# A sixth buffer for the evacuated u tiles of a fused SSM and MLP kernel

## The chip, the cores and the metric

The kernel runs on one NeuronCore of a Trainium2 chip. The metric is the time of one execution on the device in microseconds (us); less is better. Seven runs of the kernel before the change took 563.35 to 569.76 us, with a median of 567.07 us.

A core has five engines, each with its own in-order queue of instructions. TensorE (PE) multiplies matrices and writes only PSUM, which here is eight banks of 128x512 float32. ScalarE (ACT) and VectorE (DVE) read PSUM and SBUF. GpSimd (POOL) does small arithmetic on SBUF here and issues DMAs; SyncE (SP) only issues DMAs. All DMAs share the 16 DMA engines of the core. Engines wait for one another, and for DMAs, through semaphores: an instruction that waits holds up everything behind it on its own queue.

## The reference, cut to what matters

```python
def _A_ref(x, ...):                         # a diagonal state-space layer
    Lam_bar = jnp.exp(dt * Lam)
    B_bar = ((Lam_bar - 1.0) / Lam)[:, None] * Bmat
    Bu = jnp.einsum("bld,pd->blp", x + 0j, B_bar)
    for t in range(L):
        h = Lam_bar[None, :] * h + Bu[:, t, :]
        hs.append(h)
    y = 2.0 * jnp.einsum("blp,dp->bld", hseq, Cmat).real + x * Dskip[None, None, :]
def _B_ref(x, w1, b1, w2, b2):              # an MLP on the normalised x
    h = _gelu(jnp.einsum("bsd,df->bsf", _layernorm(x, axis=-1), w1) + b1)
    return jnp.einsum("bsf,fd->bsd", h, w2) + b2
g = _sigmoid((x * gate_w).sum(-1, keepdims=True))
return g * a + (1 - g) * b
```

Here L is 2048 time steps, D and P are 1024, and the MLP is 3584 wide. Everything comes in and goes out as bfloat16.

## The kernel before

**Stages.** TensorE works through four stages. First, u = B x for the real and the imaginary part of B. Then the MLP in eight blocks, "m" (x times w1, GELU) and "b" (h times w2) alternating. Last, "y" (the states times C). The scan over time runs on VectorE beside the MLP: `ssm` (L1214) handles one of 16 units (two halves of P, eight pieces of 256 steps). It loads u from DRAM, rotates it by tables, scans it, rotates it back and stores the states h to DRAM.

**A group.** All but the first few products are made by a scheme with seven products in place of eight (class `SG`, L884). A group of u is one 128-row tile `pt` of B against one half `pr` of x (two pieces of 512 steps); it is 28 matmuls in the products p1, p7, p5, p6, p2, p3 and p4. The loop at L1167 interleaves neighbouring groups: p1 of this group, p7 of the group before, p5, p6, p2, p3 of this group, p4 of the group before. A group uses three PSUM banks: `a` (two banks alternate), `e` (two alternate) and `b` (three rotate). So p1 of group n needs the bank `a` of group n-2, which is free when the u made by p2 of group n-2 has been copied out by ScalarE.

**u buffers.** `bu_group` (L1003) makes 14 groups, numbered 0 to 13 here in the order of L1164: (2,0), (3,0), (0,1), (1,1), (2,1), (3,1), (4,0), (4,1), (5,0), (5,1), (6,0), (6,1), (7,0), (7,1) as (pt, pr). The evacuated u of a group, four pieces of 128x512 bfloat16, goes to one of the 4096-byte buffers of `EVS`, and `EVN` (L948) says which buffer each group takes. `fin` (L1023) evacuates: for piece c = 0 a copy by ScalarE (L1028), for c = 1 an addition by VectorE (L1034, or L1037 and L1039 for the imaginary part). When both pieces of a part `ri` are there, `u_store` (L955) sends 256 KB of it to DRAM through the POOL queue (L958). Buffers 3 and 4 are only used by the four plain products of pt 0 and 1 at the start (L967).

**Held stores.** The normalised x is stored to DRAM (L1094) and read back by four transposing DMAs (L1061, tile `scr_xn`), which wait for the second store of group 4 (L1193). Three stores, both parts of group 5 and the first of group 6, are made to wait until these transposes are done:

```python
for m, ri in ((1, 0), (1, 1), (2, 0)):
    us_t[order[4 + m] + (ri,)].deps |= set(xn_t[:4])
```

**Memory.** `SSM` is 20480 bytes in each partition: three scan buffers of 4096 (`SB0`, L1208) and two work tiles from `SSM + 12288` on (`TM0`). A scan unit loads u into its scan buffer at L1225; units 0, 1 and 2 take the first, second and third. Before the scan starts, the first two of these are also `EVS` 3 and 4.

**Order.** The program calls nothing in a fixed order. It adds tasks with a cost, a priority and the tiles they read and write to a graph (`Graph.add`, L180). A task that writes a tile waits for all earlier readers of it. A list scheduler (L225) simulates the five queues with these costs and fixes the order on each queue; instructions and waits are then emitted in it. Priorities are 1.0 for u, 10.0 for the MLP, 49 to 52 for preparing y, and 50.0 for the scan, which so fills what VectorE has left over. A change of one dependency can move tasks on every queue.

Of the kernel before, what the change touches and what calls it, by code (L numbers as in the profile page):

```python
# [419 lines left out]
def build(nc, A_x, A_Lambda_re, A_Lambda_im, A_B_re, A_B_im, A_C_re, A_C_im, A_log_dt, A_Dskip,  # L420
# [25 lines left out]
    with es:  # L446
# [35 lines left out]
        SSM = AR.alloc(20480)  # L482
# [4 lines left out]
        BQ = [HT + 57344 + 7168 * i for i in range(3)] + [W1R, W1R + 7168]  # L487
# [4 lines left out]
        EV0 = AO + 10240  # L492
# [449 lines left out]

        b_us = [[[B("us%d_%d_%d" % (p, c, r)) for r in range(2)] for c in range(NCH // 2)] for p in range(PT)]
        b_hs = [[B("hs%d_%d" % (p, h)) for h in range(L // T)] for p in range(PT // 4)]
        EVS = [EV0, EV0 + 4096, BQ[2], SSM, SSM + 4096]
        us_t = {}
        xpose_t = {}
        EVN = (0, 1, 0, 1, 0, 1, 2, 0, 1, 2, 0, 1, 2, 0)  # L948
        US5 = B2B
        bu_n = [0]  # L950

        def u_ev(pt, pr, ks, ri, c):
            return AR.v(EVS[ks] + (ri * 4 + 2 * c) * T * 2, [(1, 2 * T)])

        def u_store(pt, pr, ks, q, ri):  # L955
            evv = AR.v(EVS[ks] + ri * 2048, [(T, 4), (1, T)])
            r0 = ((pt % 4) * 2 + ri) * T
            us_t[pt, pr, ri] = g.dma((1.0, q), lambda e: e.dma_start(out=US[pt // 4, :, 4 * pr:4 * pr + 4, r0:r0 + T], in_=evv.ap), 2 * 128 * CH * 2,  # L958
                  ssem("us", 2 * ks + ri, True), reads=[evv], writes=[b_us[pt][pr][ri]], name="us%d.%d.%d" % (pt, pr, ri), q="pool")
# [43 lines left out]
        def bu_group(pt, pr):  # L1003
            ks = EVN[bu_n[0]]

# [720 lines left out]
def bass_gated_mix__ssm_conv_s5__mixer_channel_mlp__prompt_kernel(  # L1726
    nc, A_x, A_Lambda_re, A_Lambda_im, A_B_re, A_B_im, A_C_re, A_C_im, A_log_dt, A_Dskip,
    B_x, B_w1, B_b1, B_w2, B_b2, gate_w, out,
):
    build(nc, A_x, A_Lambda_re, A_Lambda_im, A_B_re, A_B_im, A_C_re, A_C_im, A_log_dt, A_Dskip,  # L1730
          B_x, B_w1, B_b1, B_w2, B_b2, gate_w, out)
# [28 lines left out]
```

## Time and profile before

| | value |
|---|---|
| median of 7 runs | 567.07 us (563.35 to 569.76) |
| profiled execution, its own time | 566.22 us |
| its span, first to last instruction | 564.5 us |
| PE busy | 545.8 us, 97% |
| DVE busy | 521.7 us, 92% |
| ACT busy | 284.6 us, 50% |
| POOL busy | 104.2 us, 18% |
| granted TensorE clock, mean | 0.996 |

A busy engine is not in itself the limit: the table is an average over stages. What counts is which engine the others wait for at each place, and what that engine itself waits for. In the timelines a line is a run of like instructions: its start and length in us, the engine, the line of the kernel, the operation, the tiles out<-in (buffer numbers left out; `ar` is nearly all of SBUF, `ps` is PSUM, names with `scr_` are DRAM), and, in brackets, idle time before it with what ended it.

### The profile page before, as it was taken

What the parts mean: (1) busy time and instruction counts of PE and PEld (TensorE: products, weight loads), DVE (VectorE), ACT (ScalarE), POOL (GpSimd) and SP (SyncE); (2) the same over time, 40 slices, a digit from 0 to 9 for tenths busy, and PEclk for the clock granted to TensorE, in tenths of its full rate; (3) what the DMA queues carried; (4) which work ended last, traced back from release to release, by engine and by line L of the source; (5) the groups of instructions that cost most, each with busy time, mean ns of one, the idle gap of its engine ahead of it and who ended that gap; (6) DMA issues with size and microseconds to landing.
All of it is one profiled execution on the core that took longest, in us unless ns stands there. A gap on an engine that the chain in (4) does not pass through costs nothing.

```text
span 564.5 us, 7450 instructions
## 1 busy us (share of the span) xinstructions
PE 545.8 (97%) x2576; PEld 251.0 (44%) x2623; DVE 521.7 (92%) x897; ACT 284.6 (50%) x477; POOL 104.2 (18%) x152
## 2 busy tenths in 40 slices
PE   8999996999999999999999999999999999999995
PEld 6444432444444444444444444444444444444442
DVE  4899799999999999999999999999999899999752
ACT  3898876657674346674346763246763231111110
POOL 2029934623000110001210101220000210111000
PEclk9999998999999999999999999999999999999999
DMA  8999869756982664404989998998879799997501
GB/s 253 278 235 279 278 148 288 252 179 185 313 190 90 198 221 156 127 7 142 305 312 313 333 296 200 221 202 227 272 169 196 145 312 340 337 331 273 201 37 56
DMA packets 122757, 125.58 MB, mean 222 GB/s; under 512 B 70474, under 2 KB 99928, under 8 KB 121696
## 3 DMA queue, kind: packets, MB, share of 16 engines
q1 hardware_dynamic: 110256, 79.33, 49.6%
q0 software_dynamic: 12464, 45.78, 26.5%
q8 instruction: 20, 0.33, 0.2%
q14 instruction: 17, 0.14, 0.1%
HBM read 60.98 MB, written 48.38 MB: 194 GB/s over the span
## 4 chain that ended last, share of the span: by engine, by line
PE 83%; DMA 4%; SPq 4%; POOL 3%; issue 2%; ACT 2%; DVE 0%; POOLq 0%; ACTq 0%
PE ps L878 63%; PE ps L876 19%; SPq L1061 1%; DMA scr_u<-ar 1%; DMA cst<-scr_z 1%; SPq L1048 1%; DMA ar<-scr_xn 1%; POOL cst L1082 1%; DMA ar<-in_A_B_im_dram 1%; POOL cst L1087 1%; SPq L622 1%; POOL cst L1086 1%; SPq L1149 1%; POOL cst L1084 1%; ACT ar L677 0%
## 5 line engine op out<-in xcount | busy, mean ns | idle before, releaser
L878 PE MATMUL ps<-ar 128*128 128x512 f16 (+1 forms) x1793 | 412.6, 380 | 4.4 <-ACT ps L912 1.4
L878 PEld LDWEIGHTS ps<-ar 128*128 128x128 f16 (+1 forms) x1832 | 178.9, 98 | 220.3 <-ACT ps L912 2.6
L876 PE MATMUL ps<-ar 128*128 128x512 bf16 (+1 forms) x616 | 153.1, 381 | 5.3 <-ACT ar L1028 4.7
L940 DVE TENSOR_TENSOR ar<-ar 128x512 f16<-128x512 bf16 (+7 forms) x244 | 149.4, 652 | 3.6 <-ACT ar L677 2.3
L876 PEld LDWEIGHTS ps<-ar 128*128 128x128 bf16 (+1 forms) x624 | 60.9, 98 | 78.2 <-issue 6.5
L1252 DVE TENSOR_TENSOR_SCAN ar<-cst,init,ar 128x256 bf16<-128x256 f32 x128 | 88.9, 735 | 0.5
L895 ACT ACTIVATE ar<-ps 128x512 f32<-128x512 f32 x100 | 59.1, 596 | 51.0 <-PE ps L876 36.8
L1238 DVE TENSOR_TENSOR ar<-ar 128x2048 bf16<-128x2048 bf16 x64 | 77.1, 1217 | 0.1
L912 ACT ACTIVATE ps<-ps 128x512 f32<-128x512 f32 x66 | 38.6, 584 | 66.2 <-PE ps L876 61.1
L1366 ACT ACTIVATE ar<-ps,cst 128x512 bf16<-128x512 f32 x56 | 38.5, 687 | 23.7 <-PE ps L878 22.8
L896 ACT ACTIVATE ar<-ps,cst 128x512 f32<-128x512 f32 x32 | 22.0, 688 | 45.7 <-PE ps L878 23.7
L1241 DVE TENSOR_TENSOR ar<-ar 128x1024 bf16<-128x1024 bf16 x64 | 42.8, 685 | 0.3
L1449 ACT ACTIVATE ar<-ps,cst 128x512 f32<-128x512 f32 x32 | 22.0, 688 | 40.5 <-PE ps L878 40.3
L1372 ACT ACTIVATE ar<-ar,cst 128x512 bf16<-128x512 f32 x56 | 39.9, 713 | 2.2 <-DVE ar L1370 1.9
L1370 DVE TENSOR_TENSOR ar<-ps,ar 128x512 f32<-128x512 f32 x56 | 38.2, 683 | 2.8 <-PE ps L878 2.2
L1551 DVE SCALAR_TENSOR_TENSOR ar<-ps,cst,ar 128x512 bf16<-128x512 f32 x32 | 23.8, 747 | 8.6 <-PE ps L878 8.4
L958 POOL DMA_DIRECT2D scr_u<-ar x32 | 24.7, 777 | 34.1 <-DVE ar L1034 10.9
L1461 POOL DMA_DIRECT2D scr_ac<-ar x16 | 13.8, 892 | 87.6 <-DVE ar L1452 42.3
L1459 POOL DMA_DIRECT2D scr_ac<-ar x16 | 8.5, 532 | 105.1 <-DVE ar L940 36.8
L1452 DVE SCALAR_TENSOR_TENSOR ar<-ps,cst,ar 128x512 f32<-128x512 f32 x32 | 23.7, 741 | 3.4 <-PE ps L878 3.1
L1270 POOL DMA_DIRECT2D scr_h<-ar x16 | 9.7, 606 | 73.8 <-DVE ar L1241 73.7
L1558 POOL DMA_DIRECT2D out_dram<-ar x14 | 7.6, 544 | 83.1 <-DVE ar L1551 83.1
(118 smaller groups left out, 273.9 us busy)
## 6 DMA issues: line engine op xcount, KB each, us to landing
scr_ac<-ar POOLq DMA_DIRECT2D x32, 512.0 KB, 6.6
ar<-in_B_w_dram SPq DMA_DIRECT2D x21, 512.0 KB, 5.2
ar<-in_A_x_dram SPq DMA_DIRECT2D x32, 256.0 KB, 4.4
scr_u<-ar POOLq DMA_DIRECT2D x32, 256.0 KB, 4.2
ar<-scr_u SPq DMA_DIRECT2D x16, 512.0 KB, 4.5
scr_h<-ar POOLq DMA_DIRECT2D x16, 512.0 KB, 6.1
ar<-scr_h SPq DMA_DIRECT2D x8, 1024.0 KB, 7.5
ar<-scr_ac SPq DMA_DIRECT2D x16, 512.0 KB, 7.6
```

Source lines behind the costliest of these rows:

```text
L876: ins = e.matmul(V(PS[bk], 0, [(1, n)]), st[i].ap, mv[i].ap, start=(i == 0), stop=(i == K - 1))
L878: ins = e.matmul(V(PS[bk], 0, [(1, n)]), st[i].ap, mv[i].ap, start=False, stop=(i == K - 1), skip_group_check=True)
L895: return e.activation(o.ap, V(PS[bk], 0, [(1, 512)]), AF.Copy)
L912: g.add("act", c_act(512), (pb[0], q - 2), lambda e: e.activation(V(PS[b], 0, [(1, 512)]), V(PS[a], 0, [(1, 512)]), AF.Copy), reads=[b_ps[ ...
L940: g.add("dve", c_tt16(n), (pr or pb[0], q), lambda e: e.tensor_tensor(o.ap, a.ap, b.ap, op), reads=[a, b], writes=[o], name=nm, extra=ex). ...
L958: us_t[pt, pr, ri] = g.dma((1.0, q), lambda e: e.dma_start(out=US[pt // 4, :, 4 * pr:4 * pr + 4, r0:r0 + T], in_=evv.ap), 2 * 128 * CH * 2 ...
L1238: g.add("dve", c_tt16(UE), pri(i), lambda e: e.tensor_tensor(o.ap, a.ap, tbl.ap, ALU.mult), reads=[a, tbl], writes=[o], name=nm + tag)
L1241: g.add("dve", c_tt16(UE // 2), pri(i), lambda e: e.tensor_tensor(o.ap, a.ap, b.ap, op), reads=[a, b], writes=[o], name=nm + tag)
L1252: lambda e, pt=pt, ri=ri, vin=vin, go=go: e.tensor_tensor_scan(go.ap, Cb("R", pt, T), vin.ap, V(INIT, pt * 2 + ri, [(1, 1)]), ALU.mult, AL ...
L1366: g.add("act", c_act(512, ap_operands=1), (10.0, q + 1), lambda e: e.activation(o.ap, V(PS[bk], 0, [(1, 512)]), AF.Gelu_apprx_tanh, bias=C ...
L1370: g.add("dve", c_dve(512), (10.0, q - 2), lambda e: e.tensor_tensor(sv.ap, V(PS[bk], 0, [(1, 512)]), sv.ap, ALU.add), reads=[b_ps[bk], sv] ...
L1372: g.add("act", c_act(512, psum=False, ap_operands=1), (10.0, q + 3), lambda e: e.activation(o.ap, sv.ap, AF.Gelu_apprx_tanh, bias=C("B1", ...
```

## The change

The list of buffers gets a sixth entry, `SSM + 8192`, which is the third scan buffer, and the order in which the groups take buffers is written anew from group 8 on. Nothing else is edited; the planner sees other dependencies and plans all queues again.

```diff
-        EVS = [EV0, EV0 + 4096, BQ[2], SSM, SSM + 4096]
+        EVS = [EV0, EV0 + 4096, BQ[2], SSM, SSM + 4096, SSM + 8192]
         us_t = {}
         xpose_t = {}
-        EVN = (0, 1, 0, 1, 0, 1, 2, 0, 1, 2, 0, 1, 2, 0)
+        EVN = (0, 1, 0, 1, 0, 1, 2, 0, 5, 1, 2, 0, 1, 2)
```

| group | buffer before, last used by | buffer after, last used by |
|---|---|---|
| 8 | 1, group 5 | 5, nobody |
| 9 | 2, group 6 | 1, group 5 |
| 10 | 0, group 7 | 2, group 6 |
| 11 | 1, group 8 | 0, group 7 |
| 12 | 2, group 9 | 1, group 9 |
| 13 | 0, group 10 | 2, group 10 |

Scan unit 2 loads its u into `SSM + 8192`, so this load now comes after both stores of group 8.

## The prediction

> **What bounds the kernel now.** I first read the page: the share of each engine, the slices, and the chain that ended last.
>
> ```profile
> PE   8999996999999999999999999999999999999995
> ...
> PEclk9999998999999999999999999999999999999999
> ...
> PE 83%; DMA 4%; SPq 4%; POOL 3%; issue 2%; ACT 2%; DVE 0%; POOLq 0%; ACTq 0%
> ```
>
> TensorE sets the end. Between the first slice and the last there is one weak one, the seventh (84.7 to 98.8 us), and there the granted clock dips as well. In the list of waits TensorE has only one wait over 1.2 us, and the two waits behind it stand in the same list:
>
> ```profile
> POOL scr_u L958 <- DMA ar<-scr_xn: 7.6, 1, 7.6
> PE ps L876 <- ACT ar L1028: 4.7, 1, 4.7
> ACT ar L1028 <- DMA scr_u<-ar: 2.4, 1, 2.4
> ```
>
> The chain in order of time puts them in a row:
>
> ```profile
> 82.88 6.40 DMA ar<-scr_xn
> ...
> 89.89 4.30 DMA scr_u<-ar
> 94.19 0.02 issue
> 94.22 0.61 ACT ar L1028
> 94.82 0.14 issue
> 94.96 1.11 PE ps L876 x3
> ```
>
> The last transpose lands at 89.28, POOL then sends the held stores, the first lands at 94.19, ScalarE copies one u tile, TensorE goes on. Which groups are these? Every group starts with a run of L876 x4 (p1) and has a period of 6.04 us, so they can be counted in the timeline of TensorE:
>
> ```profile
> 78.01 1.03 PE L876 MATMUL ps<-ar 128*128 128x512 bf16 x4
> 84.05 1.03 PE L876 MATMUL ps<-ar 128*128 128x512 bf16 x4
> 94.96 1.54 PE L876 MATMUL ps<-ar 128*128 128x512 bf16 x4 [4.70 <-ACT ar L1028]
> 102.69 1.03 PE L876 MATMUL ps<-ar 128*128 128x512 bf16 x4
> ```
>
> These are groups 8, 9, 10 and 11. Group 10's p1 wants the bank of group 8; group 8's copy wants buffer 1, which waits for the held store of group 5. From the start of group 9 to that of group 11 it takes 18.64 us instead of 2 x 6.04: **6.56 us lost**, of which 4.70 is idle and the rest a slow restart. After 102.69 the list has no PE wait but one of PEld of 0.3 us up to the end: TensorE runs through until 557.9, so what is gained here moves the end, unless something else is late then.
>
> **The change part by part.**
>
> Group 8 goes to a buffer nobody waits for. Its copy can run when p2 ends, near 82.5, and p1 of group 10 starts at 84.05 + 6.04 = 90.1. That removes the idle 4.70 and the restart. Of the restart, the rows by microsecond show the clock:
>
> ```profile
> 94.00:95.00 1.00, 0.04 (x1) 0.07 (x2) 1.00 (x4) 0.78 (x2) 1.00 (x2) 1.00 1.02 377
> 95.00:96.00 1.00, 1.00 (x4) 0.43 (x5) 0.97 (x4) 0.87 (x2) 0.01 (x1) 0.66 1.02 377
> 96.00:97.00 1.00, 1.00 (x4) 0.32 (x3) 1.00 (x3) 0.60 (x2) 0.00 (x0) 0.50 1.02 381
> ```
>
> The column after the five engines is the granted clock: 0.50 after the wait. From 94.96 to 99.23, 12 matmuls take 4.27 us; at the steady 0.216 us each (6.04 / 28) it would be 2.59, so 1.68 us is the clock. The waits of 0.80 us (near 68) and 1.14 us (near 74) left it at 1.00. [...]
>
> Group 9 now takes buffer 1 and waits for the same held store: **what is late next.** Its copy at 94.2 frees a bank wanted by p1 of group 11, at 96.1. With the 0.61 + 0.14 us of the chain the bank is free at 94.95: 1.2 us in hand. Group 10 takes buffer 2, whose held store (group 6) leaves POOL 0.75 us later, and its bank is wanted only at 102. No stall of TensorE by these dates. But ScalarE is in order: while it waits on group 9's copy, the seed and snapshot copies of group 10 queue behind, and p6, p3 of group 10 and p4 of group 9 (92 to 95) need them. In the trace of before the planner puts group 8's copy behind three squares (L1072, 88.28 to 91.87), so it knows that the data come late, within 2.4 us. I expect it to place the seed first. Bounds 0 and 2.4 (all of ScalarE's wait); I take 0.5.
>
> Group 8's first store now leaves POOL near 84.6 (POOL is idle from 82.26 to 89.89), beside the fourth transpose. This speaks against the change. Row: the first three transposes take 2.06, 2.58 and 2.70 us of SP, the fourth 4.37 with the two stores of 80.75 in the air, so a store costs (4.37 - 2.6) / 2 = 0.9 us. [...] I take 0.9. It is within the 1.2 us in hand: nothing on TensorE, but 0.3 us are left.
>
> The three squares L1072 lose the stall as their place and go between the copies of a group. ScalarE has room (9.2 of 15 us busy from 105 to 120), but a copy that finds one running waits up to 1.06 + 0.19 us, as the 0.80 us wait behind the conversion L842 shows. Bounds 0 and 3 x 0.8; I take 0.4.
>
> The load for scan unit 2 was issued early:
>
> ```profile
> 51.75 1.29 SPq L1225 DMA_DIRECT2D ar<-scr_u  x3
> ```
>
> It is the third of these; "not yet in use" holds only because it moves. It now follows group 8's second store, sent behind the four of 89.89: near 93, landing 97. On SP it stands among the w1 loads (L1321 at 87.30 x2, 96.92, 108.83). What is queued behind it is at most w1 tiles 2 and 3, wanted by m groups 2 and 3 at 132.9 and 138.9, now 126 and 132: over 20 us of cover. Unit 2 starts rotating on VectorE after 125. Cost nothing. The slice of 512 KB moves, it isn't added.
>
> Group 13 now ends in buffer 2, at `BQ[2]`, the place of the first w2 load (SP, 133.10). That load waits for the end of m group 0 on TensorE, and now for group 13's last store as well (POOL 130.29, plus 4.2 landing = 134.5, both moved alike): 1.4 us later, and with it w1 tile 4 behind it on SP. That tile was issued at 133.54, takes 5.2 and is first read by its sums at 145.20: covered by 5 us.
>
> Sum: 6.56 - 0.5 - 0.4 = 5.7 us. From the profiled 566.22 this gives 560.5; the median of the runs is 0.85 above it, so **561.4 as a median**.
>
> **The rivals.**
>
> *VectorE becomes the bound in y (the slower side).* VectorE is full from 75 to 435. If TensorE is 6 us earlier, the scan, lowest in priority, is 6 us further behind at the start of y. Its last unit must be done with its tables before two y tiles may be loaded over them:
>
> ```profile
> 487.72 1.22 DVE L1238 TENSOR_TENSOR ar<-ar 128x2048 bf16<-128x2048 bf16 x1
> ...
> 488.96 4.47 SPq L1527 DMA_DIRECT2D ar<-scr_ac  x3
> ```
>
> That load feeds VectorE at 497 to 500 and, through it, a bank that p4 of y group 3 needs near 516. Moved, that is 510. In y VectorE spends some 10 of each 12.1 us on y itself, so 3 to 4 us of scan more take until about 493 instead of 489; the point from which TensorE stalls is about 495. [...] For it: DVE 92%. Against: 2.0 us idle at 438, which the scan can use, and 11 idle after 525. At 504 it gives 566.2 - 5.7 + 9 + 1.7 = 571, 572 as a median.
>
> [...]
>
> *The gain is given back later.* The new order brings waits of one or two us in several places of a plan that now has none (w1 sums, transposes at 158, y). At half the gain or less: 564.2 to 569, middle 566.
>
> That the stall stays though group 8 has its own buffer can only be if the new order puts the copy behind something equally late; I put that with the last.
>
> **How the numbers follow.** Forecast (560 to 562.7) 0.60; group 9 waits 0.16; given back 0.13; slower 0.11. About 0.5% (2.8 us) is what a measurement of this kernel can tell from no change: faster is below 564.2, slower above 569.9. Faster: 0.60 + 0.07 of the second = 0.67; same: 0.09 of the second and 0.12 of the third = 0.21; slower: 0.11 + 0.01 = 0.12. The range: the unknown costs reach from 0 to 4.8 us and a median can lie 1 us to either side, so from 567.07 - 6.56 - 1.5 = 559.0 up; to leave out no more than 2 in 10 it takes in most of the third case: 559 to 567.5.
>
> **What would show it.** Right: no PE wait on L1028 over 1 us between 84 and 105, the seventh slice of PE and PEclk at 9, p1 runs 6.04 us apart, m groups some 6 us earlier. The held stores leave POOL near 90, with one L958 store before them near 85. Wrong: L912 or L895 as releaser of TensorE near 93 (second case), waits after 110 (third), or y p1 runs over 12.1 us apart with L1527 late (slower).

## The result and the profile after

| | before | after |
|---|---|---|
| median of the runs | 567.16 us (562.94 to 570.04, 64 runs) | 562.92 us (559.95 to 564.34, 27 runs) |
| ratio | | 0.9921, 95% interval 0.9906 to 0.9937 |
| profiled execution, own time | 566.22 us | 563.32 us |
| its span | 564.5 us | 561.6 us |

The change is faster by 0.8%. The forecast was 561.4 as a median; for the profiled execution it was 560.5, and that took 563.32. Two runs of one kernel below, 569.17 and 571.47 us, were in a slower state with a lower mean clock (0.990 and 0.987, the other four 0.997 to 0.999), and its ratio leaves them out. The two profiled executions differ by 2.9 us, the two medians by 4.2: the runs of each kernel fall in groups some 3 us apart (the last section shows two things that can make such groups). If like is set against like, 562.94 to 564.43 became 559.95 to 560.60, and 565.74 to 567.65 became 562.43 to 564.34. That is 3.2 to 3.6 us between the medians of the groups. Before had a third group, 568.0 to 570.0, in 24 of its 64 runs; after has no counterpart, and no profile shows what that group was.

The page of the changed kernel, the rows of TensorE and of its clock over the 40 slices, and the chain that ended last by engine:

```profile
PE   8999999999999999999999999999999999999995
...
PEclk9999999999999999999999999999999999999998
...
PE 87%; DVE 3%; ACT 2%; issue 2%; SPq 2%; POOL 1%; DMA 1%; DVEq 0%; POOLq 0%; ACTq 0%
```

The weak seventh slice and its dip of the clock are gone. DMA, SP's queue and POOL, which held the stall, have shrunk in the chain from 11% to 4%, and VectorE, which had 0%, now holds 3%. That is the first sign of where the rest of the gain went. The list of TensorE's waits says the same. Its columns are the total in us, how many, and the longest:

```profile
PE ps L878 <- ACT ps L912: 2.3, 3, 1.1
...
PE ps L876 <- DVE ar L940: 1.1, 1, 1.1
```

The wait of 4.7 us on L1028 is no longer there. L912, the seed copy (ScalarE writes a start value into a PSUM bank before TensorE adds to it), has one wait more than before, where the line was:

```profile
PE ps L878 <- ACT ps L912: 1.4, 2, 1.1
```

A wait on VectorE's sums L940 is new. The timeline of TensorE shows where they stand (start, length, in brackets the idle time before):

```profile
78.45 1.03 PE L876 MATMUL ps<-ar 128*128 128x512 bf16 x4
...
90.53 1.03 PE L876 MATMUL ps<-ar 128*128 128x512 bf16 x4
...
96.58 1.03 PE L876 MATMUL ps<-ar 128*128 128x512 bf16 x4
...
101.33 1.90 PE L878 MATMUL ps<-ar 128*128 128x512 bf16 x8 [0.27 <-ACT ar L895]
...
124.84 3.63 PE L878 MATMUL ps<-ar 128*128 128x512 f16 x16 [0.89 <-ACT ps L912]
...
312.78 1.04 PE L876 MATMUL ps<-ar 128*128 128x512 f16 x4 [1.12 <-DVE ar L940]
```

Compare the starts of the p1 runs in the two timelines, group by group:

| group, p1 before | p1 after | difference | what it says |
|---|---|---|---|
| 8, 78.01 | 78.45 | +0.44 | the first loads landed later in this execution (waits of 0.95 and 1.22 us at 6.14 and 16.46 us) |
| 10, 94.96 | 90.53 | -4.43 | no idle time |
| 11, 102.69 | 96.58 | -6.11 | no slow restart either: 6.55 us removed |
| 12, 108.73 | 103.06 | -5.67 | 0.44 given back |
| m2, 132.90 | 128.30 | -4.60 | 1.07 given back, in m1 |
| m3, 138.94 | 134.48 | -4.46 | 0.14 given back, in m2 |
| 320.25 | 317.10 | -3.15 | 1.29 given back (p1 of the group before: 314.20 and 309.77) |
| end of the span | | -2.9 | 0.25 given back, behind TensorE's last product |

**The stall went whole: 6.55 of the 6.56 us. What came back is 3.2 us: 2.94 at four places, behind each of which stands VectorE, and 0.25 at the end.** At the first place and in group m1, first ScalarE's timeline, then, for m1 and the place near 312, VectorE's:

```profile
100.19 0.60 ACT L1037 ACTIVATE ar<-ps 128x512 f32<-128x512 f32 x1 [1.96 <-DVE ar L1039]
100.68 1.08 ACT L895 ACTIVATE ar<-ps 128x512 f32<-128x512 f32 x2
...
123.58 0.72 ACT L1372 ACTIVATE ar<-ar,cst 128x512 bf16<-128x512 f32 x1 [1.53 <-DVE ar L1370]
124.21 0.58 ACT L912 ACTIVATE ps<-ps 128x512 f32<-128x512 f32 x1
```

```profile
121.42 1.53 DVE L940 TENSOR_TENSOR ar<-ar 128x512 f16<-128x512 bf16 x4
122.86 0.68 DVE L1370 TENSOR_TENSOR ar<-ps,ar 128x512 f32<-128x512 f32 x1
...
309.78 2.02 DVE L1252 TENSOR_TENSOR_SCAN ar<-cst,init,ar 128x256 bf16<-128x256 f32 x3
311.73 0.66 DVE L1370 TENSOR_TENSOR ar<-ps,ar 128x512 f32<-128x512 f32 x1
312.31 1.54 DVE L940 TENSOR_TENSOR ar<-ar 128x512 f16<-128x512 bf16 x4
```

Read m1 backwards: TensorE waits for the seed (L912), the seed stands behind a GELU (L1372), the GELU waits for the sum L1370, and that stands behind four sums of a w1 tile that nobody needs yet. Near 312 TensorE waits for the sums of a w1 tile themselves, which stand behind seven scans (four at 306.26, three at 309.78). The place near 101 is of the same kind: L895 stood behind an L1037 that waited 1.96 us for VectorE's L1039. So is the small one in m2: the seed at 130.38 stood behind a GELU that waited 0.56 us for L1370. From 110 to 435 us VectorE is busy 318.6 of 325 us after and 318.4 before. While TensorE was 5.7 us later, VectorE's order had that much more room. That is an inference from the dates; the experiments test it.

### The profile page after: what moved, and what is told of

The parts are those of the page before. It is cut to its first block, busy times and chain, and to the rows that moved or that the text cites. A ratio compares the mean times of both kernels' runs of the same rounds, so it can differ in the third digit from the quotient of the medians.

```text
span 561.6 us, 7447 instructions
## 1 busy us (share of the span) xinstructions
PE 543.6 (97%) x2576; PEld 249.6 (44%) x2623; DVE 520.0 (93%) x897; ACT 284.3 (51%) x477; POOL 103.2 (18%) x152
## 4 chain that ended last, share of the span: by engine, by line
PE 87%; DVE 3%; ACT 2%; issue 2%; SPq 2%; POOL 1%; DMA 1%; DVEq 0%; POOLq 0%; ACTq 0%
PE ps L878 67%; PE ps L876 20%; SPq L1048 1%; DVE ar L1252 1%; DMA ar<-in_A_B_im_dram 1%; DVE ar L940 1%; DVE ar L1238 0%; ACT ps L912 0%; POOL scr_u L958 0%; ACT ar L1072 0%; ACT ar L677 0%; DVE ar L1370 0%; POOL cst L1083 0%; DVE ar L1039 0%; PE ps L1116 0%
## 5 line engine op out<-in xcount | busy, mean ns | idle before, releaser
L940 DVE TENSOR_TENSOR ar<-ar 128x512 f16<-128x512 bf16 (+7 forms) x244 | 149.5, 651 | 5.6 <-ACT ar L677 2.6
L895 ACT ACTIVATE ar<-ps 128x512 f32<-128x512 f32 x100 | 59.0, 596 | 47.8 <-PE ps L876 36.6
L912 ACT ACTIVATE ps<-ps 128x512 f32<-128x512 f32 x66 | 38.5, 584 | 66.1 <-PE ps L876 61.0
L1372 ACT ACTIVATE ar<-ar,cst 128x512 bf16<-128x512 f32 x56 | 40.0, 714 | 7.9 <-DVE ar L1370 7.9
L1370 DVE TENSOR_TENSOR ar<-ps,ar 128x512 f32<-128x512 f32 x56 | 38.2, 683 | 2.8 <-PE ps L878 2.4
L1452 DVE SCALAR_TENSOR_TENSOR ar<-ps,cst,ar 128x512 f32<-128x512 f32 x32 | 23.6, 741 | 1.3 <-PE ps L878 0.9
```

Of the source, the lines that this page charges most:

```text
L895: return e.activation(o.ap, V(PS[bk], 0, [(1, 512)]), AF.Copy)
L912: g.add("act", c_act(512), (pb[0], q - 2), lambda e: e.activation(V(PS[b], 0, [(1, 512)]), V(PS[a], 0, [(1, 512)]), AF.Copy), reads=[b_ps[ ...
L940: g.add("dve", c_tt16(n), (pr or pb[0], q), lambda e: e.tensor_tensor(o.ap, a.ap, b.ap, op), reads=[a, b], writes=[o], name=nm, extra=ex). ...
L1370: g.add("dve", c_dve(512), (10.0, q - 2), lambda e: e.tensor_tensor(sv.ap, V(PS[bk], 0, [(1, 512)]), sv.ap, ALU.add), reads=[b_ps[bk], sv] ...
L1372: g.add("act", c_act(512, psum=False, ap_operands=1), (10.0, q + 3), lambda e: e.activation(o.ap, sv.ap, AF.Gelu_apprx_tanh, bias=C("B1", ...
```

## The experiments

**Which part of the change does it.** The stall can be taken away by other means, and one part of the change can stand alone.

Group 8 alone gets the sixth buffer, the groups behind it keep the buffers they had before. Against the changed kernel:

```diff
-        EVN = (0, 1, 0, 1, 0, 1, 2, 0, 5, 1, 2, 0, 1, 2)
+        EVN = (0, 1, 0, 1, 0, 1, 2, 0, 5, 2, 0, 1, 2, 0)
```

> The kernel before, with group 8 alone moved to the new buffer; groups 9 to 13 keep buffers 2, 0, 1, 2, 0. If group 8's buffer is the whole cause of the stall, the wait of 4.7 us and the dip of the granted clock are gone as with the full change, and group 10 starts 6 us after group 9; what is left of the 6.56 us in the end depends on the new order of the queues, so a ratio of 0.988 to 0.995. If the rewritten order of the other groups is needed as well (rival), group 9, which waits here for a store that leaves POOL after group 5's, stalls p1 of group 11 by 2 us or more.

Measured: 564.78 us, ratio 0.9952 (0.9934 to 0.9970), span 563.2. TensorE's timeline:

```profile
90.41 1.03 PE L876 MATMUL ps<-ar 128*128 128x512 bf16 x4
...
96.59 1.04 PE L876 MATMUL ps<-ar 128*128 128x512 bf16 x4
...
99.34 1.04 PE L876 MATMUL ps<-ar 128*128 128x512 f16 x4 [0.85 <-DVE ar L1034]
```

The stall is gone with this part alone. The group behind 96.59 starts 1 us late, and further waits follow: 0.59 us on L912 at 125.14, 1.48 on VectorE's L1452 at 289.70, 0.53 on L940 at 320.41. So the sixth buffer removes the stall by itself. Whether the order of the others decides how much comes back is not settled: the interval just meets that of the change.

The kernel before, with only the other consequence of the change, the load of scan unit 2 sent after both stores of group 8:

```diff
-                  ssem("sb", s), reads=[b_us[4 * pg + a][q // 4] for a in range(4)], writes=[uf], name="ul" + tag)
+                  ssem("sb", s), reads=[b_us[4 * pg + a][q // 4] for a in range(4)], writes=[uf], name="ul" + tag, extra=[us_t[5, 0, 0], us_t[5, 0, 1]] if un == 2 else ())
```

> The kernel before, with one dependency added: the load of scan unit 2 waits for both stores of group 8, as in the changed kernel; buffers as before. If moving this load costs nothing, the stall at group 10 stays at 4.7 us and the time stays within 0.5% of before, ratio 0.995 to 1.005. If the moved load is what gives back the missing 2 us (rival), the ratio is 1.003 to 1.005 and unit 2 starts late on VectorE.

Measured: 567.93 us, ratio 1.0001 (0.9984 to 1.0018). The stall stands, with 3.92 us of idle time before 94.59, and no wait is new behind it. The moved load (it left at 104.31) costs nothing that these runs can tell, which is 1 us. In this execution the restart took longer than before; the last section comes back to it.

The kernel before without the hold:

```diff
-                        us_t[order[4 + m] + (ri,)].deps |= set(xn_t[:4])
+                        pass
```

> The kernel before, without the hold: the stores of group 5 and the first of group 6 go out when their data are ready; buffers as before. If the hold is what makes group 8's buffer late, the wait of 4.7 us is gone here too and the ratio is like that of the change, 0.988 to 0.995; the transposes, with three more stores of 256 KB beside them, end 3 x 0.9 = 2.7 us later than 89.3. If the stores take more than that from the transposes (rival: the hold protects something), what reads the transposed tiles is late and the ratio is 1.0 or more.

Measured: 563.85 us, ratio 0.9945 (0.9925 to 0.9964), span 562.0. The p1 runs of groups 8 to 12 are 6.04 us apart (77.90, 83.94, 89.99, 96.03, 102.07). With five buffers the stall goes as well, so the held stores were its cause. The rival, that the hold protects the transposes, is not borne out: they took 11.43 us of SP against 11.95 with the hold. And again something comes back, in three places: 1.16 us on L912 at 124.12, 1.48 on L1452 at 288.58, 0.53 on L940 at 319.28.

The kernel before with a shorter hold, for three transposes in place of four:

```diff
-                        us_t[order[4 + m] + (ri,)].deps |= set(xn_t[:4])
+                        us_t[order[4 + m] + (ri,)].deps |= set(xn_t[:3])
```

> The kernel before, with the held stores waiting for three of the four transposes only. The hold ends some 3 us sooner, so the wait of TensorE is 1 to 2.5 us instead of 4.7. [...] The gain of the stall is then 4 to 5.5 us, less what the new order gives back: ratio 0.990 to 0.998.

Measured: 568.15 us, ratio 1.0018 (0.9993 to 1.0043). The wait on L1028 fell from 4.70 to 2.23 us and the clock stayed at 1.00, yet the kernel is no faster: 0.45 us on L1034, 1.07 on L895, then 0.79, 0.46, 0.65 and 0.32 us at 136 to 155 and 0.34 and 0.24 near 320 take what was won. The 4 to 5.5 us expected reckon with no slow restart: this run shows none, but behind a wait of 2.02 us in another the clock stood at 0.50 (last section). From group 9 to group 11 this execution gained 2.3 us on the kernel before (84.85 to 101.19 in place of 84.05 to 102.69), and by the p1 run of 413.37 (before: 410.90) it had lost 4.0. Here more came back than had been won.

**Whether what came back can be won.** The first try was to let the planner do it. Three kernels from the changed one: the load of w1 tile 11 is given a shorter planned duration, so that its sums are placed sooner; the second GELU of group m0 is told to come later, so that the seed of m1 goes before it; and both.

```diff
-                  D * 256 * 2, ssem("w1", s), writes=[o], name="w1_%d" % j, bw=DMA_BW_512, extra=ex)
+                  D * 256 * 2, ssem("w1", s), writes=[o], name="w1_%d" % j, bw=DMA_BW_512 * (2 if j == 11 else 1), extra=ex)
```

> The changed kernel, with the planner told that the load of w1 tile 11 is twice as fast; nothing of the computation or of the DMA itself changes, only the order of the queues. If the 1.3 us lost at m group 11 come from the order in which VectorE was told to work (the four sums of the tile behind seven scans), the wait of TensorE on L940 near 312 is gone or under 0.3 us and the time is 0.5 to 1.3 us under that of the changed kernel: ratio to before 0.989 to 0.992. If VectorE is simply full there (rival), the wait turns up within 30 us of that place, at a like size, and the ratio stays at 0.992.

```diff
-                          reads=[sv, bc("B1")], writes=[o], name="gelu" + nm)
+                          reads=[sv, bc("B1")], writes=[o], name="gelu" + nm).slack = 1.0 if (jj, c) == (0, 0) else 0.0
```

> The changed kernel, with the second GELU of m group 0 planned 1 us later, so that ScalarE does the seed copy of m group 1 before it. If the 1.1 us lost at m group 1 are ScalarE's order alone, the wait on L912 near 124.8 is gone and 0.9 to 1.1 us are won: ratio 0.990 to 0.992. If VectorE, late against the plan, is the cause (rival), the wait moves to the next instruction that needs its addition (p3 or p4, releaser L1372 or L1370) and less than 0.4 us is won.

> The changed kernel with both of these edits. If both waits are matters of order, their gains add up: 1.9 to 2.4 us under the changed kernel, ratio 0.987 to 0.990. If VectorE is the limit (rival), other waits on VectorE's results take their place and the ratio stays at 0.991 to 0.993.

Measured: 564.39, 563.52 and 563.87 us (ratios 0.9945, 0.9936 and 0.9939). None is better than the change alone. In the first the wait at 312 fell to 0.29 us, in the second the seed's wait of 0.89 us turned up one group later as 0.78, and in the third as 1.03. And in the first two a wait appeared that the prediction had weighed: group 9's copy, with the held store. POOL's timeline and ScalarE's in the first of the three:

```profile
91.58 2.23 POOL L958 DMA_DIRECT2D scr_u<-ar  x3 [3.20 <-DMA ar<-scr_xn]
```

```profile
96.82 2.01 ACT L1028 ACTIVATE ar<-ps 128x512 bf16<-128x512 f32 x3 [1.56 <-DMA scr_u<-ar]
```

In the changed kernel these stores left at 90.13 and the copies ran at 95.34. Here the transposes were done 1.4 us later, and the p1 of group 11 waited 0.91 us (0.52 in the second). SP and POOL work in the same order as in the changed kernel up to there, and the four transposes took 12.44 us of SP in place of 9.68. So the margin that was called 1.2 us is thin, and the changed kernel may itself miss it in some executions; its profile does not show that.

These kernels were planned anew as a whole, so they can't say whether VectorE's time or only its order is at fault. The next one keeps the order of every engine and shortens two sets of sums in it; it leaves out the rest of these sums (all but 8 of their 512 columns):

```diff
-            dve_tt("w1a%d" % j, q, sq(0), raw(1, 0), raw(1, 1), ALU.add, 512)
+            dve_tt("w1a%d" % j, q, sq(0), raw(1, 0), raw(1, 1), ALU.add, 512, cut=8 * (j in (3, 11)))
...
```

> The changed kernel, instruction for instruction in the same order, with the four w1 sums of weight tiles 3 and 11 cut from 512 to 8 elements a partition (the rest of those sums is left out, so the output is not the reference's). Each set of four is 1.53 us on VectorE; at the 0.16 us of an 8-element operation it would be about 0.6. Theory (what the change gave back is VectorE arriving late in program order): the wait of 0.89 us at 124.84 falls to 0 to 0.2, the wait of 1.12 us at 312.78 to 0 to 0.3, no new wait appears since no order changes, and the time falls by 1.5 to 2.1 us, to about 561.0 (ratio near 0.989). Rival 1 (the sums are beside the point: the GELU and the seed on ScalarE are late by themselves, or the w1 load is): both waits stay as they are, 562.9. Rival 2 (whatever is gained there is waited for at the next place, as in the three reorderings): the two waits go, others of the same sum appear before 330 us, and the time stays within 0.5 us of 562.9.

Measured: 562.01 us (561.87 to 562.41), ratio 0.9907 (0.9886 to 0.9928), span 560.3 against 561.6. VectorE's timeline, then TensorE's:

```profile
121.40 0.56 DVE L940 TENSOR_TENSOR ar<-ar 128x8 f16<-128x8 bf16 x4
121.89 0.68 DVE L1370 TENSOR_TENSOR ar<-ps,ar 128x512 f32<-128x512 f32 x1
```

```profile
127.32 1.03 PE L876 MATMUL ps<-ar 128*128 128x512 bf16 x4
...
311.53 1.04 PE L876 MATMUL ps<-ar 128*128 128x512 f16 x4 [0.86 <-DVE ar L940]
```

In m1 L1370 comes 0.97 us sooner, the wait is gone, and p1 starts at 127.32 in place of 128.30: what VectorE saved, TensorE gained. At the second place the sums were shortened by 1.0 us and TensorE gained only 0.26 more. It starts there once the first of the four sums is done (in the changed kernel that one runs from 312.31 to 312.72, TensorE from 312.78), and only what that one saved counts; the rest of the wait is its place behind seven scans. Nothing of the 1.24 us was given back until the end. The theory holds for the first place in full and for the second in kind, with its size wrong.

So the order was then changed by hand at just these two places, with all the work done: the sums of tile 3 go behind the two L1370, those of tile 11 ahead of three scans.

```diff
         g.schedule(horizon=HORIZON)
+        dv = g.order["dve"]
...
+        move(["w1a3", "w1c3", "w1b3", "w1d3"], "cadd0.0.3")
+        move(["w1a11", "w1c11", "w1b11", "w1d11", "cadd10.1.3"], "cadd10.1.1")
```

> The changed kernel, whole, every engine's order as it was but for two places on VectorE: the four w1 sums of tile 3 stand behind the two L1370 sums that GELU waits for (they stood ahead of them), and the four w1 sums of tile 11 stand ahead of three scans (they stood behind them). The same work, nothing planned anew. Theory (the loss behind 120 us is VectorE's order at these two places): the wait of 0.89 us at 124.84 and the wait of 1.12 us at 312.78 both go (0 to 0.2 us each), group m1 and the group behind 317.10 start 1.0 and 2.2 to 2.3 us sooner, no new wait; time 560.6 to 561.2, ratio near 0.988. Rival (VectorE is full there, what it does sooner for one it does later for another): waits of the same sum on VectorE's scans, on L1370 or on the y sums appear behind these places, and the time stays within 0.5 us of 562.9.

Measured: 561.50 us (6 runs, the four that count in the ratio 560.22 to 562.28), ratio 0.9895 (0.9855 to 0.9934), an interval that overlaps that of the change. By the median alone the theory seems right. But three of the four lie at 560.22 to 560.72, where the lower group of the change lies (559.95 to 560.60), and the trace does not bear it out:

```profile
127.84 3.63 PE L878 MATMUL ps<-ar 128*128 128x512 f16 x16 [0.77 <-ACT ps L912]
...
316.04 3.61 PE L878 MATMUL ps<-ar 128*128 128x512 f16 x16 [0.65 <-ACT ps L912]
...
328.29 1.04 PE L878 MATMUL ps<-ar 128*128 128x512 f16 x4 [0.22 <-DVE ar L1370]
```

The two waits went, and three others came behind them, the first two just one group on. At 316.04 the GELU ahead of the seed waited 1.16 us for the L1370 at 313.97, which now stands behind the scans that were put off and 2.33 us of other sums. This execution was 2.91 us ahead of the changed kernel's at the p1 run before these places (118.28 against 121.19; the last section says why), and VectorE was ahead by as much (its scans at 115.32 against 118.23). It was ahead by 3.24 us at the p1 run of 404.51 (against 407.75). Of the 2.2 us that the theory expected in between, 0.33 were won. **The rival fits: what VectorE does sooner for one, it does later for another.** Less work helped; none of the orders tried did. That no order can is not shown: the L1370 at 313.97, for one, could go ahead of those 2.33 us of sums.

**Whether the hold still costs.** The changed kernel without the hold, with half of it, and without it and with VectorE's order changed by hand at three places:

```diff
-                        us_t[order[4 + m] + (ri,)].deps |= set(xn_t[:4])
+                        pass
```

> The changed kernel with the held stores let go as well (they no longer wait for the first four transposes). Theory (with the sixth buffer the hold costs nothing more, and the rest of the loss lies on VectorE): no wait at the p1 products of groups 8 to 13, as already in the changed kernel but for 0.4 us; VectorE's order is planned anew and waits of 0.5 to 1.5 us in all appear behind 120 us; 562 to 563.5. Rival (the hold is worth something, it keeps the stores off the transposes): the transposes take more than the 9.7 us they take in the changed kernel, VectorE's scan starts later, and the time is above 564.

```diff
-                        us_t[order[4 + m] + (ri,)].deps |= set(xn_t[:4])
+                        us_t[order[4 + m] + (ri,)].deps |= set(xn_t[:2])
```

> The changed kernel, the held stores waiting for the first two transposes in place of four. Theory: the margin of group 11's copy to its buffer (in two of the reorderings it was late by 0.5 to 0.9 us) grows by some 2 us, so no p1 product waits; waits behind 120 us as VectorE's new order has them, 0.5 to 1.5 us; 561.5 to 563.5. Rival (each plan trades these waits against each other and none is free of them): a wait of 1 us or more in the m groups, 563.5 or above.

```diff
         g.schedule(horizon=HORIZON)
+        dv = g.order["dve"]
...
+        move(["w1a3", "w1c3", "w1b3", "w1d3"], "cadd0.0.3")
+        move(["ac0.7.3"], "sc4.0.0")
+        move(["w1a12", "w1c12", "w1b12", "w1d12"], "cadd11.1.1")
```

> The changed kernel without the hold (the kernel of the run with six buffers and no hold, 564.0 us), with VectorE's order changed at the three places where its products waited: the sums of tile 3 behind the two L1370, one L1452 ahead of two scans, and the sums of tile 12 ahead of a 2-us weight sum. Theory: the waits of 1.15 us at 123.62, 1.48 us at 288.07 and 0.53 us at 318.78 go (0 to 0.2 us each), 2.6 to 3.2 us in all; time 560.8 to 561.6, ratio near 0.989. Rival (VectorE is full): the waits come up elsewhere and the time stays within 0.5 us of 564.0.

Measured without the hold: 564.00 us, ratio 0.9941 (0.9921 to 0.9961), above the 562 to 563.5 expected, with the same three waits as the kernel before without the hold (1.15, 1.48 and 0.53 us). Without the hold the sixth buffer shows no gain (563.85 with five). With half of it: 565.68 us, ratio 0.9980 (0.9960 to 1.0000), with 2.02 us on L912 at 126.18. Without it and by hand: 561.88 us (560.88 to 565.38, 8 runs), ratio 0.9919 (0.9884 to 0.9953). In its profiled execution from the p1 run at 121.34 to that at 409.61 it takes 288.27 us, and without the changes by hand 288.06 (119.72 to 407.78). Nothing was won there either: waits of 1.24 us at 131.72, 0.56 at 288.93, 0.41 at 296.20 and 1.00 at 323.27 stand in place of the three. Its runs fall in two groups, 560.88 to 561.91 and 564.31 to 565.38, and the profiled one is of the upper; the runs without the changes by hand all lie at 563.30 to 564.64. So the lower median comes from the share of the groups, and the order is not shown to have won anything. No kernel of this study with all its work is shown to be faster than the change.

## Why the prediction was right

**The stall and its size.** Predicted: 6.56 us lost, 4.70 of it idle and the rest a slow restart, all of it gone with the sixth buffer. Measured: 6.55 us removed, and the granted clock at 1.00. The rows are those of the changed kernel: window, us, TensorE busy, clock, DMA share, GB/s.

```profile
90.00:95.00 5.00, 4.95 (x24) 1.00 1.11 345
95.00:96.00 1.00, 1.00 (x7) 1.00 1.01 377
```

**The terms taken off it were wrong in place and in size.** 0.5 us was for ScalarE waiting on group 9's copy and 0.4 us for the three squares. Neither was paid: the p1 runs from group 8 to group 11 are 6.04 to 6.05 us apart, and no copy L1028 waits for a store. What was given back came from VectorE, 2.94 us at four places, with 0.25 more at the end, against 0.9 in the sum. The step that missed is "TensorE runs through until 557.9, so what is gained here moves the end": half of it did. The prediction had this as a rival ("the gain is given back later"), with w1 sums among its examples and a chance of 0.13; it put the price at half of the gain or more. The signs that it gave for being right came (no wait on L1028, the slices at 9, p1 runs 6.04 us apart), and so did its sign for that rival, waits after 110. In the profiled pair 2.9 of the forecast 5.7 us remain, about the half that this rival named. The median, 562.92, lies just above the forecast case (560 to 562.7) and below that rival's 564.2; that it came so near the forecast of 561.4 is in part luck, because the runs before have the group of 568 to 570 us that those after lack. The mechanism was named and its price belonged in the sum: that VectorE is full from 75 to 435 us had been read and was used for one rival only.

**What is late next.** Predicted: group 9's copy at 94.2, 1.2 us in hand. Measured: 95.34, of which 0.44 is the later start of this execution; on ScalarE it stood behind one of the squares L1072 (93.82) and an L895. With 0.75 us for the copy and the step to TensorE, the bank was free 0.5 us before group 11's p1. Two of the reorderings went past it by 0.5 and 0.9 us. The case that group 9 waits (0.16) was close, though not by a seed queued behind the copy: group 11's p1 was what waited.

**The store beside the fourth transpose.** Predicted: leaving at 84.6, costing 0.9 us within those 1.2. POOL's timeline of the changed kernel:

```profile
87.08 1.49 POOL L958 DMA_DIRECT2D scr_u<-ar  x2 [4.38 <-DVE ar L1034]
90.13 2.23 POOL L958 DMA_DIRECT2D scr_u<-ar  x3 [1.57 <-DMA ar<-scr_xn]
```

It left 2.5 us later than predicted, since VectorE's L1034 for it was late in its own queue, and the held stores left at 90.13, which is 0.2 us earlier than before once the 0.44 is taken off. In sum the term was nothing, but not as a proof that a store costs nothing: the fourth transpose took 7.1 us to land in place of 6.40, and it had been issued 0.9 us sooner, for which no run shows the reason. The row for 0.9 us a store was misread: the fourth transpose, with the same two stores in the air, held SP for 3.03 us here in place of 4.37.

**Loads that move.** Unit 2's load went from the run at 51.75 to 98.46 and cost nothing that shows, as in the run with that load alone (1.0001). The w2 load went out at 128.57 and nothing waits for it.

**The slower rival.** VectorE's last scan unit and the load that waits for it, VectorE's timeline first, then SP's:

```profile
485.99 1.22 DVE L1238 TENSOR_TENSOR ar<-ar 128x2048 bf16<-128x2048 bf16 x1
```

```profile
487.23 4.77 SPq L1527 DMA_DIRECT2D ar<-scr_ac  x3
```

It was expected near 493 with a stall from 495 on; it came 1.73 us sooner than before, while TensorE came 3.15 us sooner: the scan fell behind by 1.4 us, not by 6. The argument had TensorE run ahead of a full VectorE by 6 us; in the trace TensorE waits for VectorE at four places on the way instead, and half of that lead is gone before y begins. The 1.7 us in that rival's sum are the 1.68 us of the restart at 94.96 in the kernel before; the changed kernel's list of waits has none of TensorE's from 435 us to the end, so no run shows that term there.

## What to carry to other kernels

When a stall is taken from the engine that sets the end, look at the engine that is second. Here it was busy 98% of the stretch behind, the stall was its slack, and about half of the gain came back as short waits on whatever stood in its queue ahead of what was now needed sooner. Put a price on that from the start. To see whether such waits can be won, change that engine's work in an order that is otherwise kept, and only then its order; compare start times in two traces, since a median of six runs can seem to confirm what the trace does not show.

## What the runs showed of the hardware

**Behind a wait of 2.02 us the clock stood at half, behind one of 2.23 us at full.** The first stands in the kernel with six buffers and half of the hold (idle from 124.16 to 126.18), the second in the kernel before with the hold for three transposes (idle from 91.05 to 93.28). TensorE of the first kernel in the stretch at half the clock and in the ones before and behind it (the column after the busy time is the clock):

```profile
122.80:126.22 3.42, 1.40 (x8) 1.00 0.42 108
126.22:129.63 3.41, 3.41 (x9) 0.50 0.26 77
129.63:133.04 3.41, 3.41 (x17) 1.00 0.11 10
```

And of the second, in stretches of the same length:

```profile
91.28:94.70 3.42, 1.42 (x7) 1.00 1.12 350
94.70:98.11 3.41, 2.91 (x14) 1.00 1.05 401
```

So the clock fell behind the shorter of the two waits and not behind the longer; what decides it, these two do not show.

In the first kernel the run of sixteen that follows took 5.31 us in place of 3.62, as much (1.69) as the restart cost in the kernel before: one stretch of 3.41 us at half the clock (95.32 to 98.74 there). In the kernel with the scan load moved (idle from 90.67 to 94.59) it was twice that, 6.82 us:

```profile
90.28:93.70 3.42, 0.39 (x2) 1.00 1.14 335
93.70:97.11 3.41, 2.52 (x7) 0.50 0.99 326
97.11:100.52 3.41, 3.41 (x10) 0.50 0.98 284
100.52:103.94 3.42, 3.37 (x16) 1.00 0.68 227
```

There the clock fell at 93.70, while the wait still ran. From p1 of group 10 to p1 of group 11 it took 8.96 us, against 7.73 in the kernel before and 6.04 without a slow restart. So the stall at group 10 cost 1.7 us on top of its wait in one of these executions and 2.9 in the other. From these two, as an estimate, executions of the kernel before can differ by 1.2 us through this alone.

**Two GpSimd instructions of 4 elements a partition took 4.94 us in one trace and 1.33 in another.** They are the first two L1085, powers, in the norm's small chain. POOL's timeline of the changed kernel, then VectorE's, which at last waits for the end of that chain:

```profile
52.63 4.94 POOL L1085 TENSOR_TENSOR cst<-cst 128x4 f32<-128x4 f32 x2
```

```profile
52.67 1.21 DVE L816 TENSOR_TENSOR ar<-ar,cst 128x1024 f32<-128x1024 f32 x1
...
56.68 0.68 DVE L1039 TENSOR_TENSOR ar<-ar 128x512 bf16<-128x512 f32 x1
57.28 0.68 DVE L1034 TENSOR_TENSOR ar<-ps,ar 128x512 bf16<-128x512 f32 x1
...
62.12 4.01 DVE L1092 TENSOR_SCALAR ar<-ar,cst 128x1024 bf16<-128x1024 bf16 x8 [3.03 <-POOL cst L1087]
```

The first of the two took 4.79 us. From 52.67 to 57.28 VectorE runs five operations in a row with both inputs in SBUF. Then comes L1034, which takes one input from PSUM, and 0.14 us after its start the long L1085 ends. In 12 of the 14 traces the two L1085 take 4.93 or 4.94 us together and end 0.29 to 0.31 us after an L1034 has begun. These are dates; no run took those operations away, so what makes the L1085 long is not shown.

The same in the kernel with sums moved by hand, whose instructions stand in the same order there:

```profile
52.55 1.33 POOL L1085 TENSOR_TENSOR cst<-cst 128x4 f32<-128x4 f32 x2
```

```profile
59.19 4.01 DVE L1092 TENSOR_SCALAR ar<-ar,cst 128x1024 bf16<-128x1024 bf16 x8 [0.16 <-POOL cst L1087]
```

Here the two L1085 took 1.33 us, with the same operations on VectorE (52.59 to 57.22); why is open. VectorE starts L1092 2.93 us sooner, TensorE's waits of 0.80 us at 69.29 and 1.14 us at 74.93 do not occur, and group 8's p1 comes at 75.82 in place of 78.45. The 2.6 us fit the distance between the groups of runs (560 and 563 after), so it is likely that this makes them; of the profiles only this one is of a group near 560, and it was not tested by itself. The other kernel in which L1085 was short, that without the hold and with changes by hand, spent 4.64 us on the two L1082 just ahead (1.96 in the kernel with sums moved by hand), and its profile is of an upper group. For a prediction it means that some 2.6 us of this kernel's time may be decided from one run to the next, and that two kernels should be compared within the same group.
